# A recurrent attention kernel with a SoLU block behind it: another order for the blocks' inverses, and 32-blocks one round earlier

## The chip, the cores and the metric

The kernel runs on one core of a Trainium2 chip. The core has five engines that work in parallel, each through its own queue in program order: PE (TensorE, matrix products; PEld is its weight load), DVE (VectorE), ACT (ScalarE), POOL (GpSimd) and SP (SyncE, which here only issues transfers). They wait for one another through semaphores. Transfers between HBM and the core's SBUF are issued by SP, ACT or POOL and carried by 16 DMA engines. PE writes to PSUM, from which DVE or ACT must copy a result out before its bank can be used again.

The metric is the device time of one execution in microseconds. All inputs and outputs are 32-bit floats, or 64-bit for the weights that the kernel narrows itself.

## What is computed

A linear recurrence with a state of 40 x 40 for each of 4 x 8 heads and 768 positions, and behind it, on the 3072 rows of 320 that it gives, a block with a softmax-weighted hidden layer of 1024:

```python
for t in range(S):                                   # S = 768, D = 40
    y[:, :, t] = einsum('bhd,bhde->bhe', rt, state)
    Sa = einsum('bhde,bhe->bhd', state, at)
    state = state * wt[:, :, None, :] - einsum('bhd,bhe->bhde', Sa, bt)
    state = state + einsum('bhd,bhe->bhde', vt, kt)
...
h = x @ w_in                                         # 320 -> 1024
solu = h * softmax(h)
ln = (solu - mean(solu)) / sqrt(var(solu) + 1e-06) * g_ln
out = ln @ w_out                                     # 1024 -> 320
```

## The kernel before

**Tiling.** The 768 positions are cut into 12 chunks of L = 64. A *round* n is one chunk of all four batches; it holds two *steps*, i = 2n and 2n + 1, each with two batches, so there are 24 steps. Inside a chunk the recurrence becomes products, and the inverse of a triangular 64 x 64 matrix for each head. That matrix is called nt; its diagonal has two 32 x 32 blocks (Q = 32).

**The inverse.** The diagonal blocks of one round (64 heads and halves) are written to HBM by `scatter` (L424) and fetched again by `gather` as one block per partition. `invert` then eliminates column by column on DVE, two instructions for each column. For rounds below FINE = 4 (L23), `gather` (L434) and `invert_fine` work on blocks of 16: a set-up (L447, L448), then 14 pairs of L456 (prod) and L458 (u), two ACT copies (L462), and a write to HBM (L464). `solve` then has to join two 16-blocks on PE: products py16, DVE L602 (y), products pz16, and six ACT copies (L613, L618). From round FINE on, the blocks are 32 wide: `gather` by L439, set-up L476, L478, L480, then 30 pairs of L486 and L488, a write by L492, and nothing to join. Round 0's first step is inverted by doubling on PE instead, with DVE evictions L584, L589 and L593.

`bring_inverse(n)` (L499, four transfers on SP) brings round n's inverse into the one buffer tinvT. `solve` reads it first with a DVE transpose (L598) into tinv, then makes py and pz (L547), which ACT evicts (L629, L633).

**The order.** Nothing is left to a scheduler. Each stage is a generator, and `turns` takes a string of letters and advances the generator of each letter by one `yield`: f and g are `front` (decay factors and nt of a later step), a is `attend` (step i + 1: transposes kT, vT and rT, products psi and lamv, x), s is `solve` (step i + 1), I the inverse of a later round, r `recurrence` (step i), y `readout` (step i, ends with DVE L730), W the narrowing of the weights (L179 to L191), h `hidden`, o and b `output` and the rest of `hidden` for step i - LAG (LAG = 6). In `more` a letter has a count of yields, here `inverse_steps(i)` for I. Steps 0 to 5 use EARLY (L829; step 0 the second string, since it has two fronts), step 6 CENTRE (L832), later ones STEADY and LATE. So the order of instructions on every engine is written out by hand, and an instruction that waits holds up all behind it on its engine.

**Transfers.** `load(n, names)` issues two transfers for each of the inputs w, b, a, k, v, r of round n on SP (L335). In odd steps B stands for `arrivals`, which issues `bring_inverse` for the next round and then `gather` for the one after it; X is `repack` (L741 to L744), which turns the step's result into xT. At the end of step 0 the program has `scatter(2)`, then load(3, "k") and load(1, "r"); B of step 1 comes after them. `store` (L812) writes a round's output in two halves.

PSUM: transposes and small products share two banks ("bank"), so a product waits until the one two before it has been evicted; wide ones share two pairs of banks ("duo").

## Time and profile before

Five executions took 678.15 to 680.65 us, with a median of 679.33. The profiled execution took 675.67 us; its span from the first to the last instruction is 673.6 us.

| what | value |
|---|---|
| median of 5 executions | 679.33 us |
| profiled execution: time, span | 675.67 us, 673.6 us |
| mean granted TensorE clock | 0.968 of full speed |
| largest DMA queue (q1, issued by SP) | 45.80 MB, 39.9% of 16 engines' span |
| L488, DVE u, 32-blocks | x240, 66.6 us |
| L486, DVE prod, 32-blocks | x240, 65.8 us |
| L547, PE py | x1280, 24.1 us busy |
| DVE L598 waiting for tinvT by DMA | 27.7 us in 11 waits, longest 8.2 us |

The page also draws the span in 40 equal slices of 16.8 us; a digit is the busy share in tenths, and PEclk the granted clock:

```profile
PE   7697678798888999999999999999999999999996
PEld 4575566577666677677667667766766666555554
DVE  4549567487797696786887876976966844424433
ACT  3254545556445244334534433453442334412312
POOL 4414313132221121121112112111200100000000
PEclk9988867989899999999999999999999999999999
```

PE is busy nearly all the time from about the thirteenth slice on. In the first twelve, which hold the start-up and steps 0 to 6, it is not, and the clock is often below full speed. A step lasts 20 to 34 us in this part. Idle time of an engine costs something only where a chain of waits passes through it; the chain of work that ended last and the timeline say where.

### The profile page before, as it was taken

The numbers are of one execution on the slowest core, as the hardware profiler recorded it, in microseconds if no ns is written. First come the engines' busy times: TensorE is split into PE (matmuls) and PEld (weight loads), VectorE is DVE, ScalarE is ACT, GpSimd is POOL, SyncE is SP. The second block draws the span as 40 slices with busy tenths as digits, with TensorE's granted clock in tenths as the row PEclk, the third lists the DMA queues.
The fourth block names the chain that finished last, engine by engine and source line by source line (L and its number), as shares of the span: only waits on it lengthen the run. The fifth ranks groups of instructions, "written<-read, shape, count | busy, mean of one in ns | idle before, by whom it ended". The sixth has DMA issues, their size and how long they took to land.

```text
span 673.6 us, 28595 instructions
## 1 busy us (share of the span) xinstructions
PE 611.7 (91%) x12579; PEld 433.0 (64%) x12579; DVE 444.6 (66%) x1203; ACT 275.5 (41%) x663; POOL 119.1 (18%) x219
## 2 busy tenths in 40 slices
PE   7697678798888999999999999999999999999996
PEld 4575566577666677677667667766766666555554
DVE  4549567487797696786887876976966844424433
ACT  3254545556445244334534433453442334412312
POOL 4414313132221121121112112111200100000000
PEclk9988867989899999999999999999999999999999
DMA  9769648457362456454454543553334120000000
GB/s 157 107 149 151 120 82 134 90 110 134 84 105 50 97 80 119 66 97 86 74 93 88 89 80 84 84 93 82 39 76 78 25 42 19 21 24 20 19 21 19
DMA packets 238155, 53.74 MB, mean 80 GB/s; under 512 B 227400, under 2 KB 235344, under 8 KB 238032
## 3 DMA queue, kind: packets, MB, share of 16 engines
q1 hardware_dynamic: 232928, 45.80, 39.9%
q0 software_dynamic: 1696, 5.25, 3.1%
q8 instruction: 99, 1.62, 1.1%
q10 hardware_dynamic: 3408, 0.87, 0.9%
q14 instruction: 24, 0.20, 0.1%
HBM read 36.95 MB, written 10.22 MB: 70 GB/s over the span
## 4 chain that ended last, share of the span: by engine, by line
PE 67%; DVE 15%; ACT 8%; issue 5%; DMA 3%; SPq 1%; ACTq 1%; POOL 0%; DVEq 0%
PE po L799 16%; PE h L754 13%; PE pyo L723 4%; PE py L547 3%; PE pz L547 3%; PE plnT L794 3%; PE pcx L370 3%; DVE prod L486 2%; DVE u L488 2%; PE pcum L357 2%; PE plamv L308 2%; PE ppsi L308 2%; DVE nmax L764 2%; PE plamu L308 2%; DMA tinvT<-u_dram 2%
## 5 line engine op out<-in xcount | busy, mean ns | idle before, releaser
L754 PE MATMUL h<-w_in,xT 128*128 128x512 f32 (+1 forms) x288 | 124.9, 624 | 0.0
L799 PE MATMUL po<-w,lnT 128*128 128x320 f32 x384 | 115.9, 440 | 3.2 <-ACT lnT L795 3.2
L799 PEld LDWEIGHTS po<-w,lnT 128*128 128x128 f32 x384 | 68.3, 190 | 29.2 <-ACT lnT L795 5.8
L488 DVE TENSOR_TENSOR u<-u,prod 128x30 f32<-128x30 f32 (+7 forms) x240 | 66.6, 278 | 8.2
L486 DVE TENSOR_TENSOR prod<-blk,u 128x30 f32<-128x30 f32 (+7 forms) x240 | 65.8, 274 | 7.0
L764 DVE TENSOR_REDUCE nmax<-h 128x1 f32<-128x1024 f32 x24 | 29.3, 1221 | 52.5 <-PE h L754 52.5
L360 POOL TENSOR_TENSOR kx<-raw_b,inv 128x320 f32<-128x320 f32 x24 | 20.9, 869 | 232.6 <-ACT inv L358 218.7
L754 PEld LDWEIGHTS h<-w_in,xT 128*128 128x128 f32 (+1 forms) x288 | 38.0, 188 | 29.7 <-issue 27.7
L804 ACT ACTIVATE osb<-po,rs 128x320 f32<-128x320 f32 x24 | 12.6, 527 | 98.9 <-PE po L799 87.3
L795 ACT COPY lnT<-plnT 128x512 f32<-128x512 f32 x48 | 27.0, 587 | 41.2 <-PE plnT L794 41.1
L786 POOL TENSOR_TENSOR rs<-c,mhalf 128x1 f32<-128x1 f32 x24 | 13.2, 549 | 151.8 <-DVE c L785 150.7
L547 PE MATMUL py<-tinv,nt 32*32 32x32 f32 x1280 | 24.1, 200 | 15.7 <-DVE tinv L598 14.0
L311 DVE TENSOR_TENSOR lamv<-plamv,cst 128x512 f32<-128x512 f32 x24 | 16.6, 690 | 29.6 <-PE plamv L308 29.6
L771 DVE TENSOR_TENSOR e<-h,e 128x1024 f32<-128x1024 f32 x24 | 29.4, 1224 | 10.0 <-ACT e L768 9.4
L370 PE MATMUL pcx<-cst,lw 128*128 128x132 f32 x192 | 33.2, 300 | 3.1 <-DVE y L602 1.5
L768 ACT ACTIVATE e<-h,nmax 128x1024 f32<-128x1024 f32 x24 | 26.8, 1115 | 20.6 <-DVE nmax L764 15.3
L370 PEld LDWEIGHTS pcx<-cst,lw 128*128 128x128 f32 x192 | 27.5, 200 | 11.7 <-ACT y_mid L629 3.5
L633 ACT ACTIVATE tinvT<-pz 32x256 f32<-32x256 f32 x48 | 17.9, 373 | 39.9 <-PE pz L547 39.6
L372 ACT ACTIVATE kx<-pcx 128x264 f32<-128x264 f32 x48 | 18.8, 392 | 36.8 <-PE pcx L370 36.6
L547 PEld LDWEIGHTS py<-tinv,nt 32*32 32x32 f32 x1280 | 20.5, 113 | 20.3 <-issue 16.4
L709 POOL TENSOR_TENSOR sm<-tot,fac 128x320 f32<-128x320 f32 x20 | 14.8, 741 | 101.6 <-DVE tot L708 60.1
L730 DVE TENSOR_TENSOR x<-pyo,kx 128x512 f32<-128x512 f32 x24 | 16.2, 674 | 23.0 <-PE pyo L723 22.9
(139 smaller groups left out, 1192.5 us busy)
## 6 DMA issues: line engine op xcount, KB each, us to landing
blk<-blk_dram SPq DMA_DIRECT2D x16, 256.0 KB
raw_k<-in_k_dram SPq DMA_DIRECT2D x24, 160.0 KB
v<-in_v_dram SPq DMA_DIRECT2D x24, 160.0 KB
r<-in_r_dram SPq DMA_DIRECT2D x24, 160.0 KB
out_dram<-osb SPq DMA_DIRECT2D x24, 160.0 KB
raw_w<-in_w_dram SPq DMA_DIRECT2D x23, 160.0 KB
raw_b<-in_b_dram SPq DMA_DIRECT2D x23, 160.0 KB
raw_a<-in_a_dram SPq DMA_DIRECT2D x23, 160.0 KB
```

The source lines that it names most:

```text
L308: nc.tensor.matmul(t[half(c ^ p * cross), p, g * L:(g + 1) * L], lhsT=lhs[half(p), g, half(c)], rhs=rhs[half(p), g, half(c)], start=True, ...
L370: nc.tensor.matmul(t[:, g * 132:g * 132 + 132], lhsT=pair(lw, 2 * j + g), rhs=cst[:, lo:lo + 132], start=True, stop=True)
L486: nc.vector.tensor_tensor(out=t, in0=nb[:, j:j + 1, j + 1:Q].to_broadcast([P, rows, m]), in1=u[:, 0:rows, j:j + 1].to_broadcast([P, rows, ...
L488: nc.vector.tensor_tensor(out=u[:, 0:rows, j + 1:Q], in0=u[:, 0:rows, j + 1:Q], in1=t, op=ALU.subtract)
L547: nc.tensor.matmul(t[quarter(out), c:c + Q], lhsT=lhs(p, g), rhs=rhs(p, g), start=True, stop=True)
L723: nc.tensor.matmul(t[half(p), c, g * W:g * W + used], lhsT=kb[half(c), j, 2 * g + p, :], rhs=lam[half(c), h % 2, h // 2, 0:used], start=i ...
L754: nc.tensor.matmul(h[:, j * 512:j * 512 + 512], lhsT=of_round[i // 2]["xT"][rows, kt, i % 2 * P:i % 2 * P + P], rhs=w_in[rows, 4 if kt == ...
L764: nc.vector.tensor_reduce(out=nmax, in_=h, axis=AX.X, op=ALU.max, negate=True)
L768: nc.scalar.activation(out=e, in_=h, func=AF.Exp, bias=nmax, accum_out=esum)
L771: nc.vector.tensor_tensor(out=q, in0=h, in1=e, op=ALU.mult)
L795: nc.scalar.copy(out=lnT[:, fs.start:fs.stop].rearrange("p f t -> p (f t)"), in_=t)
L799: nc.tensor.matmul(o[:, 0:DM], lhsT=lnT[:, f, :], rhs=w2[:, f, :], start=f == 0, stop=f == NF - 1)
```

## The change

The diff touches the order and the size of blocks in the first third of the kernel and one transfer at the end:

- FINE becomes 3: round 3 (steps 6 and 7) is gathered, inverted and brought as 32-blocks, and solves 6 and 7 have nothing to join. `inverse_steps` gives 17 yields to step 3 and 15 to step 4, as the 32 yields need, where the 16-block inverse had 8 and 8.
- Load(3, "k") and load(1, "r") move from the end of step 0 into `arrivals` of step 1: k between `bring_inverse(1)` and `gather(2)`, r behind `gather(2)`.
- In step 0 the first yields of round 1's inverse stand behind one `a` and one `s` more, and there are 4 of them instead of 5, with 6 instead of 5 in the next place.
- In the start-up, `solve(0)` and the inverse of round 0 alternate otherwise, and one `s` moves from the third string into the second.
- CENTRE has two `s` less.
- The second half of the last round's store is issued by ACT.

```diff
-FINE = 4
+FINE = 3
...
-            nc.sync.dma_start(out=rows[:, 2 * c:2 * c + 2, :], in_=of_round[n]["osb"][half(c)])
+            (nc.scalar if c and n == NCH - 1 else nc.sync).dma_start(out=rows[:, 2 * c:2 * c + 2, :], in_=of_round[n]["osb"][half(c)])
...
-             "r r a r W f r r W g W s y r W a f g L W a I a s f g W a I s f g W I s a f g W I s f g W I")
+             "r r a r W f r r W g W s y r W a f g L W a a s I f g W a I s f g W I s a f g W I s f g W I")
...
-    CENTRE = "r r a r f o I r o r o s y o r X I o h a f L a s a h I f s a h I f s h f s h I a f h"
+    CENTRE = "r r a r f o I r o r o s y o r X I o h a f L a s a h I f a h I f s h f h I a f h"
...
         if i == 0:
-            return [5, 5, 5, 1, 0]
+            return [4, 6, 5, 1, 0]
...
         if i < LAG:
+            if i in (3, 4):
+                return [0, 0, 4, 4, 4, 5] if i % 2 else [5, 4, 4, 2, 0, 0]
             return [0, 0, 2, 2, 2, 2] if i % 2 else [3, 3, 1, 1, 0, 0]
...
             bring_inverse(n)
+        if i == 1:
+            load(3, "k")
         if n + 1 < NCH:
             gather(n + 1)
+        if i == 1:
+            load(1, "r")
...
-        turns("f g s f s * g a s f I s I f a s I g I s I g a I", dict(I=[2, 3, 3, 3, 3, 99]), f=f, g=g, s=so, a=at, I=inv,
+        turns("f g s f s * g a s f s I f a s I g I s I I g a s I", dict(I=[2, 3, 3, 3, 3, 99]), f=f, g=g, s=so, a=at, I=inv,
...
-        turns("s f W s * f a s a g s g f g W W", {}, f=f, g=g, s=so, a=at, W=ws, **{"*": warmer})
+        turns("f W s * f a s a g s g f g W W", {}, f=f, g=g, s=so, a=at, W=ws, **{"*": warmer})
...
-            if i == 0:
-                load(3, "k")
-                load(1, "r")
```

## The prediction

> **What bounds the kernel now.** I began with the page's busy shares and its chain of what ended last, since they say whether one engine or a relay of engines sets the end.

> ```profile
> PE 611.7 (91%) x12579; PEld 433.0 (64%) x12579; DVE 444.6 (66%) x1203; ACT 275.5 (41%) x663; POOL 119.1 (18%) x219
> ...
> PE 67%; DVE 15%; ACT 8%; issue 5%; DMA 3%; SPq 1%; ACTq 1%; POOL 0%; DVEq 0%
> ```

> PE holds two thirds of the chain, but DVE and DMA hold a fifth, and the 40 slices put their part in the first third. So I cut the span at L730, the last VectorE product of each step. L730 starts at 54.04 us in step 0, 88.10 in step 1, and so on to 222.32 in step 7. The busy times between these marks, in the order length, PE, PEld, DVE, ACT, POOL, granted clock, DMA share, GB/s:

> ```profile
> 88.10:111.50 23.40, 20.47 (x580) 17.30 (x581) 17.42 (x61) 11.88 (x34) 4.11 (x8) 0.72 0.66 111
> ...
> 134.28:154.59 20.31, 18.88 (x587) 15.04 (x588) 17.05 (x61) 11.31 (x33) 6.79 (x13) 0.92 0.56 111
> 154.59:175.82 21.23, 17.52 (x590) 13.85 (x587) 12.73 (x37) 12.84 (x35) 5.24 (x9) 1.00 0.69 135
> 175.82:197.05 21.23, 18.13 (x584) 14.75 (x586) 19.89 (x62) 9.51 (x26) 3.73 (x6) 0.92 0.43 80
> ...
> 222.32:246.57 24.25, 23.41 (x459) 16.72 (x460) 20.67 (x59) 9.89 (x23) 4.10 (x7) 1.00 0.53 94
> ```

> The last row shows that from step 8 PE is busy 23.41 of 24.25 us: time won or lost before 222 us reaches the end unchanged. In the fourth row DVE is busy 19.89 of 21.23 us; that step holds the start of the first 32-block inverse, and DVE sets its length. The second row is the step into which the change puts 32-blocks, and DVE is at 17.05 of 20.31 there already.

> Third, the timeline around the longest stall. Columns: start, length, engine, line, operation, count, idle time before it and its releaser.

> ```profile
> 76.02 1.37 SPq L335 DMA_DIRECT2D raw_k<-in_k_dram  x2
> 77.43 1.60 SPq L335 DMA_DIRECT2D r<-in_r_dram  x2
> 79.56 5.23 SPq L499 DMA_DIRECT2D tinvT<-u_dram  x4
> 84.83 2.02 SPq L434 DMA_DIRECT2D blk<-blk_dram  x2
> ...
> 87.46 0.71 DVE L598 STREAM_TRANSPOSE tinv<-tinvT 128x512 f32<-128x512 f32 x1 [8.16 <-DMA tinvT<-u_dram]
> ...
> 88.32 1.08 PE L547 MATMUL py<-tinv,nt 32*32 32x32 f32 x64 [8.87 <-DVE tinv L598]
> ...
> 91.57 1.11 PE L289 MATMUL prT<-cst,r 128*128 128x128 f32 x4
> ```

> SP issues four loads, then round 1's inverse; DVE waits 8.16 us for it, PE 8.87.

> **The change part by part.** The sum is made against the profiled execution (675.67 us, span 673.6) and then moved to the median, 679.33, which lies 3.66 higher.

> *Inverse of round 1 ahead of k(3) and r(1): -3.8 us.* L499 would start at 76.02. From first issue to L598, where L598 waited, took 6.4 us (127.23 to 133.65), 5.25 (169.93 to 175.18) and 3.3 (218.53 to 221.79), so L598 can run at 79.3 to 82.4 instead of 87.46. But what was ahead is now behind. The four L499 need 1.95 us to issue, the k loads 1.4, so gather L434 starts near 79.4. Its other awaited row took 4.8 us (22.23 to 27.07), so the blocks are there at 84.2, and L447, which stands in the DVE queue ahead of L602, waits for them. The r load starts near 81.4; k loads, the nearest rows for a landing, took 5.5 us (24.60 to 30.07) and 6.4 (76.02 to 82.38). With 6.4, since the queue is as full, prT runs at 87.8 instead of 91.57: -3.8. Behind prT on PE stand pz of solve 2 and all that follows, so prT decides. Bounds: L598 alone counts, at 79.3, -8.2; or r, now the last of the four, lands when the last of them, the gather, is used now (89.46), which leaves 2.1, of which the half clock takes 0.6: -1.5.

> *32-blocks in steps 3 and 4: +8.8 us.* Between the marks of steps 3 and 4 DVE has 13 pairs of L456 and L458 with the set-up L447. The changed DVE order has set-up L476 to L480 and 25 pairs of L486 and L488 in their place, everything else (four narrowed weight pieces, five masks) being the same. Old, start to start: 0.9 + 13 x 0.46 = 6.9 us. New, from the first 32-inverse in the trace: set-up 177.08 to 179.02, 1.9 us; 25 pairs from 0.45 us (128x30) to 0.65 (128x128), 14.3 us. DVE waited 2.3 us in the 20.31 (lamu 1.0, lamv 0.6, kx 0.5, nt 0.2) and was taken for the other 18.0. New length 18.0 - 6.9 + 16.2 = 27.3, +7.0; pairs that ran beside POOL took up to 0.8 longer (200 us), which gives up to +8.7. I take +7.3. The cover is only the 2.3 us of waits, and it is used up. After the mark, L602 of step 4 stood behind one pair (156.79 to 157.75); now behind four, 1.8 us plus the same stretch of 0.6: +1.5, and prT and pz wait for L602 there, so it passes on. Bounds 0 to 2.

> *The clock in the longer step: +0.8 us.* PE has no more work in 27 us, so it idles in pieces. Before 176.04 it idled 1.99 us, and the following row has clock 0.92, 1.7 us of full rate lost. One such drop may fall in steps 3 and 4, on PE's part of the chain or beside it: between 0 and two drops, 3.4; I take half of one.

> [...]

> *What steps 5 and 6 no longer do: -3.4 us.* Solves 6 and 7 lose py16, pz16, six ACT copies and L602, and their L598 moves 256 instead of 512 columns (0.44 against 0.71 us). The ACT copies are hidden. From 175.82 to 205 DVE does not wait, so each instruction counts: L598 twice and L602 twice, 0.26 each, 1.0. Then:

> ```profile
> 203.06 0.72 PE L370 MATMUL pcx<-cst,lw 128*128 128x132 f32 x4 [1.52 <-DVE y L602]
> ...
> 205.64 0.69 DVE L311 TENSOR_TENSOR lamv<-plamv,cst 128x512 f32<-128x512 f32 x1 [0.36 <-PE plamv L308]
> ...
> 210.97 1.22 DVE L764 TENSOR_REDUCE nmax<-h 128x1 f32<-128x1024 f32 x1 [2.03 <-PE h L754]
> ```

> PE's wait of 1.52 for L602 goes, with about 1.9 us of products (py16 0.6, pz16 1.3), so both DVE waits, 0.36 and 2.03, go too. 1.0 + 0.4 + 2.0 = 3.4; bounds 2 and 4.

> *Last store's second half on ACT's queue: -0.5 us.* After the last L804 the two L812 take 1.25 us to issue one behind the other; in parallel 0.6 is saved, bounds -0.65 and +0.3.

> *Nothing:* (a) Start-up and step 0. DVE gets the same instructions in another order up to L401 at 65.39, and DVE is full from 50 to 65. In the start-up L602 slips by some 0.6 us behind two more pairs, beside a paT that ends then anyway, and round 0's L464, two loads and L499 by 1.7; solve 1 reads the result only at 53.4. Bounds -1.0 and +0.8. (b) Gather 3 and round 3's u in other shapes: L439 issued in 1.93 us at 172.04, L434 took 3.10 at 129.34; L492 took 1.28 at 213.46, and SP waits at 162 to 167 for nt anyway. (c) The two "s" gone from CENTRE: solve 7 is exhausted by then.

> Sum: -3.8 + 7.3 + 1.5 + 0.8 - 3.4 - 0.5 = +1.9 us. 675.67 becomes 677.6; 679.33 becomes **681.2**.

> **The rivals.** *The round-1 stall goes whole (faster).* If blocks and r land by 83 us, prT follows py directly (3.2 us behind it, as now) and PE has no second idle, so that part of the low clock of 0.72 after the mark goes as well. The place is solve 2 in step 1, the price 8.2 and about 1 of clock, 9.2, and it decides from a gain of 5.7, r landing by 85.9. Then the sum with 7.3 + 1.5 - 3.4 - 0.5 and no clock term is -4.3: 675.0. For it: 8.16 us of wait is a lot, and SP's issue of L499 was slowed (5.23 against 1.95 elsewhere) by the loads ahead. Against it: the same slow queue now carries gather and r.

> *Round 3 loses the clock too (slower).* DVE-bound step 3 leaves PE at 18.9 of 27 us; after the mark of step 1 PE was at 20.5 of 23.4 and the clock still 0.72. Two drops on the path and the upper price of the pairs: +3.4 instead of 0.8 and +8.7 instead of 7.3 give +5.9: 685.2. Against it: step 5, also bound by DVE, kept 0.92.

> *The first part does nothing (slower).* The wait turns from L598 into L447 and prT, with r at 90.5 us: -1.0 instead of -3.8 gives +4.7: 684.0. For it: ten transfers (four L499, two each of k, blocks and r) must now land before prT, where eight did. Against it: the two rows of a k load say 5.5 and 6.4 us after issue, not 9.

> **How the numbers follow.** Within 0.2%, 1.4 us, is about what a measurement of this kernel can't tell from no change. Forecast 0.45, its own range 679 to 683.5; a third of it lies within 1.4 us. Whole stall gone 0.33, clock lost 0.15, first part idle 0.07. Faster 0.33; same 0.15; slower 0.30 + 0.15 + 0.07 = 0.52. The range reaches down to the first rival and up past the second: 674.9 to 686.0.

> **What would show it.** L598 of step 1 at 79 to 82 us, with L447 and prT waiting in turn for DMA. From the mark of step 3 to that of step 4 27 to 29 us, DVE without waits. Step 5 shorter by 0.5, step 6 by some 2.5 to 3. I am wrong if DVE's pairs in step 3 run beside waits larger than 2.3 us, or if prT starts before 85.

## The result, and the profile after

The changed kernel took 681.51 us in the median of 44 executions (675.80 to 685.98), the kernel before 678.81 in 79 that lay beside them (671.51 to 685.32). The ratio is 1.0049, 95% interval 1.0034 to 1.0063: 3.3 us slower (the two medians differ by 2.7). A single execution of either kernel scatters by a few us, so in what follows ratios are used for what a change is worth, and profiles for where the time lies. The profiled execution of the changed kernel took 683.05 us, with a span of 680.8.

From its page, the busy shares, the clock in 40 slices and the chain of what ended last:

```profile
PE 614.6 (90%) x12259; PEld 435.7 (64%) x12259; DVE 449.7 (66%) x1235; ACT 271.9 (40%) x649; POOL 118.4 (17%) x217
...
PEclk9889869798779999999999999999999999999999
...
PE 63%; DVE 18%; ACT 5%; issue 5%; SPq 4%; DMA 3%; ACTq 0%; POOL 0%; DVEq 0%; POOLq 0%
```

DVE's part of the chain rose from 15 to 18%, SP's queue from 1 to 4%, and the clock in the tenth to twelfth slice (153 to 204 us) fell from 9, 8 and 9 tenths to 8, 7 and 7. The time between the marks (L730 of one step to L730 of the next):

| steps | before | after | difference |
|---|---|---|---|
| start to 0 | 54.04 | 54.89 | +0.8 |
| 0 to 1 | 34.06 | 29.95 | -4.1 |
| 1 to 2 | 23.40 | 24.86 | +1.5 |
| 2 to 3 | 22.78 | 23.17 | +0.4 |
| 3 to 4 | 20.31 | 27.08 | +6.8 |
| 4 to 5 | 21.23 | 25.55 | +4.3 |
| 5 to 6 | 21.23 | 22.09 | +0.9 |
| 6 to 7 | 25.27 | 22.49 | -2.8 |
| 9 to 23 | 323.24 | 322.95 | -0.3 |

The busy times of the changed kernel in these stretches; columns: start and end, length, PE, PEld, DVE, ACT, POOL with their instructions, granted clock, DMA share, GB/s:

```profile
84.84:109.70 24.86, 19.76 (x583) 16.39 (x583) 17.56 (x61) 11.91 (x35) 4.98 (x9) 0.76 0.66 109
132.87:159.95 27.08, 20.03 (x592) 15.36 (x591) 24.56 (x86) 11.95 (x35) 6.29 (x11) 0.94 0.56 106
159.95:185.50 25.55, 22.45 (x586) 18.45 (x586) 14.05 (x44) 12.00 (x33) 5.25 (x9) 0.73 0.53 96
185.50:207.59 22.09, 16.88 (x424) 13.54 (x426) 19.12 (x61) 8.05 (x21) 3.56 (x6) 0.85 0.44 75
207.59:230.08 22.49, 20.91 (x451) 15.12 (x452) 18.11 (x47) 9.56 (x22) 4.03 (x7) 1.00 0.47 79
```

The second row (step 3 to 4) has DVE busy 24.56 of 27.08 us, where it had 17.05 of 20.31: that is the 32-block inverse. The third row (step 4 to 5) is the surprise. DVE has 14.05 us to do in 25.55, PE is busy 22.45 at a clock of 0.73; before, the same step had PE at 17.52 us and a clock of 1.00. PE has about as many products as before (586 against 590) and is busy 4.9 us longer with them.

The timeline of the changed kernel around round 1; columns: start, length, engine, line, operation, count, idle time before it and its releaser:

```profile
77.15 3.69 SPq L499 DMA_DIRECT2D tinvT<-u_dram  x4
80.89 1.39 SPq L335 DMA_DIRECT2D raw_k<-in_k_dram  x2
82.38 2.10 SPq L434 DMA_DIRECT2D blk<-blk_dram  x2
84.20 0.71 DVE L598 STREAM_TRANSPOSE tinv<-tinvT 128x512 f32<-128x512 f32 x1 [4.80 <-DMA tinvT<-u_dram]
84.52 1.66 SPq L335 DMA_DIRECT2D r<-in_r_dram  x2
85.06 1.07 PE L547 MATMUL py<-tinv,nt 32*32 32x32 f32 x64 [5.58 <-DVE tinv L598]
86.32 0.86 POOL L360 TENSOR_TENSOR kx<-raw_k,inv 128x320 f32<-128x320 f32 x1 [4.41 <-DMA raw_k<-in_k_dram]
87.13 0.29 DVE L447 TENSOR_SCALAR u<-blk 128x256 f32<-128x256 f32 x1 [0.84 <-DMA blk<-blk_dram]
90.50 1.08 PE L289 MATMUL prT<-cst,r 128*128 128x128 f32 x4 [2.12 <-DMA r<-in_r_dram]
```

L598 came at 84.20 instead of 87.46, with a wait of 4.80 instead of 8.16 us. But L447 now waits for the blocks and prT for r, and prT starts at 90.50 instead of 91.57. Measured from the mark of step 0 it came 1.9 us earlier. POOL's L360, which reads k of round 3, now waits 4.41 us for it; POOL's next instruction then waits 1.89 us for DVE, so nothing on POOL is held up by that.

### The profile page after: what moved, and what is told of

It is laid out like the page before. It is cut to its first block, busy times and chain, and to the rows that moved or that the text cites. A ratio compares the mean times of both kernels' runs of the same rounds, so it can differ in the third digit from the quotient of the medians.

```text
span 680.8 us, 27973 instructions
## 1 busy us (share of the span) xinstructions
PE 614.6 (90%) x12259; PEld 435.7 (64%) x12259; DVE 449.7 (66%) x1235; ACT 271.9 (40%) x649; POOL 118.4 (17%) x217
## 3 DMA queue, kind: packets, MB, share of 16 engines
q0 software_dynamic: 1696, 5.25, 3.1%
## 4 chain that ended last, share of the span: by engine, by line
PE 63%; DVE 18%; ACT 5%; issue 5%; SPq 4%; DMA 3%; ACTq 0%; POOL 0%; DVEq 0%; POOLq 0%
PE po L799 16%; PE h L754 13%; PE pyo L723 4%; DVE prod L486 4%; DVE u L488 3%; PE plnT L794 3%; PE pcx L370 2%; PE pz L547 2%; PE py L547 2%; PE pcum L357 2%; DVE nmax L764 2%; PE plamv L308 2%; PE ppsi L308 2%; PE pyo L645 2%; PE plamu L308 2%
## 5 line engine op out<-in xcount | busy, mean ns | idle before, releaser
L754 PE MATMUL h<-w_in,xT 128*128 128x512 f32 (+1 forms) x288 | 124.9, 624 | 0.0
L488 DVE TENSOR_TENSOR u<-u,prod 128x120 f32<-128x120 f32 (+4 forms) x270 | 73.9, 274 | 9.3
L486 DVE TENSOR_TENSOR prod<-blk,u 128x120 f32<-128x120 f32 (+4 forms) x270 | 74.1, 274 | 7.8
L764 DVE TENSOR_REDUCE nmax<-h 128x1 f32<-128x1024 f32 x24 | 29.3, 1220 | 50.4 <-PE h L754 50.4
L360 POOL TENSOR_TENSOR kx<-raw_b,inv 128x320 f32<-128x320 f32 x24 | 21.0, 874 | 238.9 <-ACT inv L358 211.0
L754 PEld LDWEIGHTS h<-w_in,xT 128*128 128x128 f32 (+1 forms) x288 | 38.0, 188 | 29.7 <-issue 27.7
L804 ACT ACTIVATE osb<-po,rs 128x320 f32<-128x320 f32 x24 | 12.7, 527 | 98.6 <-PE po L799 87.1
L311 DVE TENSOR_TENSOR lamv<-plamv,cst 128x512 f32<-128x512 f32 x24 | 16.5, 688 | 32.0 <-PE plamv L308 32.0
L547 PE MATMUL py<-tinv,nt 32*32 32x32 f32 x1152 | 23.1, 200 | 14.5 <-DVE tinv L598 7.8
L370 PE MATMUL pcx<-cst,lw 128*128 128x132 f32 x192 | 33.3, 302 | 0.8 <-ACT vT L291 0.5
L370 PEld LDWEIGHTS pcx<-cst,lw 128*128 128x128 f32 x192 | 27.9, 202 | 8.7 <-ACT y_mid L629 3.7
L547 PEld LDWEIGHTS py<-tinv,nt 32*32 32x32 f32 x1152 | 19.6, 114 | 18.8 <-issue 9.3
L776 DVE BATCH_NORM_STATS2 bs<-e 128x6 f32<-128x512 f32 x48 | 30.8, 684 | 0.6
L730 DVE TENSOR_TENSOR x<-pyo,kx 128x512 f32<-128x512 f32 x24 | 16.1, 673 | 22.3 <-PE pyo L723 22.2
```

The costliest lines, as they stand in the source:

```text
L370: nc.tensor.matmul(t[:, g * 132:g * 132 + 132], lhsT=pair(lw, 2 * j + g), rhs=cst[:, lo:lo + 132], start=True, stop=True)
L486: nc.vector.tensor_tensor(out=t, in0=nb[:, j:j + 1, j + 1:Q].to_broadcast([P, rows, m]), in1=u[:, 0:rows, j:j + 1].to_broadcast([P, rows, ...
L488: nc.vector.tensor_tensor(out=u[:, 0:rows, j + 1:Q], in0=u[:, 0:rows, j + 1:Q], in1=t, op=ALU.subtract)
L547: nc.tensor.matmul(t[quarter(out), c:c + Q], lhsT=lhs(p, g), rhs=rhs(p, g), start=True, stop=True)
L754: nc.tensor.matmul(h[:, j * 512:j * 512 + 512], lhsT=of_round[i // 2]["xT"][rows, kt, i % 2 * P:i % 2 * P + P], rhs=w_in[rows, 4 if kt == ...
L764: nc.vector.tensor_reduce(out=nmax, in_=h, axis=AX.X, op=ALU.max, negate=True)
```

## The experiments

Ratios are always to the kernel before, taken beside the same runs, with 95% intervals; they are not the quotients of the medians.

### Which part costs: the change without 32-blocks, the 32-blocks alone, the loads alone

```diff
(the changed kernel, no 32-blocks in round 3)
-FINE = 3
+FINE = 4
-            if i in (3, 4):
-                return [0, 0, 4, 4, 4, 5] if i % 2 else [5, 4, 4, 2, 0, 0]
```

> The changed kernel with 16-blocks in round 3 again (32-blocks from round 4 on, as before); the moved loads, the start-up orders, CENTRE and the last store stay as changed. Theory A (the steps of the prediction: the loads gain, the 32-blocks of steps 3 and 4 cost more than steps 5 and 6 give back): the loads -3.8 by the prediction's sum, or about -2.2 by the marks of the two profiles (step 0 to 1 -4.1, the two steps behind it +1.9), the store -0.5, so 674.5 to 676.6 us, ratio to the kernel before 0.993 to 0.996; step 3 to 4 back at 20 to 21 us and step 6 to 7 back at 25. Theory B (the 32-blocks are neutral in the whole and the loss is in the loads and the start-up, where half clock moved from one place to another): as slow as the changed kernel, 681 us or more, ratio 1.003 or more.

Measured: 675.39 us, ratio 0.9971 (0.9948 to 0.9994). Step 3 to 4 took 21.41 us and step 6 to 7 24.41. Without the 32-blocks the change is a gain of 2.0 us, so theory B is out; the gain is smaller than theory A had it, whose range the interval still reaches.

```diff
(the kernel before, 32-blocks in round 3 alone)
-FINE = 4
+FINE = 3
+            if i in (3, 4):
+                return [0, 0, 4, 4, 4, 5] if i % 2 else [5, 4, 4, 2, 0, 0]
```

> The kernel before with 32-blocks in round 3 and their step lists alone. Theory A: step 3 to 4 takes 27 us (+7), step 4 to 5 2 to 4 longer with half clock behind the late L602, step 6 to 7 some 2.8 shorter: +5.2 by the prediction's terms (7.3 + 1.5 - 3.4, with no clock), up to +8 with the clock that the marks show, so 684.5 to 687.5 us, ratio 1.008 to 1.012. Theory B: the 32-blocks give back what they take: ratio 0.998 to 1.002.

Measured: 681.56 us, ratio 1.0066 (1.0032 to 1.0100), 4.5 us. Its busy times from the marks of steps 3, 4 and 6, columns as above:

```profile
130.17:158.70 28.53, 21.22 (x592) 16.66 (x592) 25.63 (x87) 11.93 (x35) 6.43 (x11) 0.88 0.63 116
158.70:180.62 21.92, 19.06 (x583) 15.38 (x584) 14.14 (x45) 11.39 (x32) 5.24 (x9) 0.84 0.48 88
...
202.69:225.20 22.51, 20.70 (x451) 15.19 (x452) 18.12 (x47) 9.57 (x22) 4.03 (x7) 1.00 0.51 90
```

DVE fills step 3 to 4 again, and step 6 to 7 is again 2.8 us shorter; the first is far larger than the second. Theory A is right in kind, its lower end a little high. Its 2 to 4 us for step 4 to 5 are not in this profile: the step took 21.92 us, 0.7 longer than before, at a clock of 0.84, although PE waited as long for L602 as in the changed kernel:

```profile
163.79 0.77 PE L547 MATMUL pz<-tinvT,y 32*32 32x32 f32 x63 [2.26 <-DVE y L602]
```

```diff
(the kernel before, the two loads moved as in the change)
@@ arrivals
             bring_inverse(n)
+        if i == 1:
+            load(3, "k")
...
             gather(n + 1)
+        if i == 1:
+            load(1, "r")
@@ end of step 0
-                load(3, "k")
-                load(1, "r")
```

> The kernel before with only k of round 3 and r of round 1 moved behind the inverse of round 1. Theory A: L598 of step 1 at 80 to 84 us, prT waits for r; -3.8 by the prediction's sum, about -2 if the new wait for r keeps PE at half clock and the steps 1 to 3 give half of it back; 675.5 to 677.3 us, ratio 0.9945 to 0.997. Theory B: the wait only changes its name, prT no earlier than 90.5 us and the mark of step 3 where it was: ratio 0.999 to 1.002.

Measured: 677.15 us, ratio 1.0031 (0.9999 to 1.0064). (The medians, 677.15 beside 677.88, differ a little the other way; the 3.8 us of the prediction would be a ratio of 0.9944.) Neither theory had this: L598 and prT came earlier, and the kernel was not measurably faster. The timeline of this kernel:

```profile
81.67 0.71 DVE L598 STREAM_TRANSPOSE tinv<-tinvT 128x512 f32<-128x512 f32 x1 [4.24 <-DMA tinvT<-u_dram]
82.34 1.64 SPq L335 DMA_DIRECT2D r<-in_r_dram  x2
84.93 0.29 DVE L447 TENSOR_SCALAR u<-blk 128x256 f32<-128x256 f32 x1 [1.17 <-DMA blk<-blk_dram]
88.14 1.09 PE L289 MATMUL prT<-cst,r 128*128 128x128 f32 x4 [2.29 <-DMA r<-in_r_dram]
```

The same two new waits as in the changed kernel. Step 0 to 1 took 29.03 us (-5.0), step 1 to 2 25.03 (+1.6) at a clock of 0.75, and step 4 to 5 25.37, where the profile before has 21.23. So the moved loads by themselves bring no gain that could be measured, where the prediction had -3.8.

### Why step 4 grew: the late L602, or the clock behind it

In the changed kernel PE waited 2.26 us for L602 in step 4 (it belongs to solve 5, which runs there). The wait, and the granted clock in the stretches around it:

```profile
165.03 1.08 PE L547 MATMUL pz<-tinvT,y 32*32 32x32 f32 x64 [2.26 <-DVE y L602]
```

```profile
161.70:165.10 3.40, 1.14 (x42) 0.84 (x37) 3.16 (x12) 0.94 (x2) 1.77 (x3) 1.00 0.34 68
165.10:178.70 13.60, 13.60 (x309) 11.70 (x310) 6.50 (x22) 6.43 (x19) 1.69 (x4) 0.50 0.39 75
```

For 3.40 us PE was busy a third of the time; for the 13.60 us after that it ran at half clock without a pause. Two experiments take this apart. The first removes what made L602 late, four pairs ahead of it on DVE:

```diff
(the changed kernel)
-                return [0, 0, 4, 4, 4, 5] if i % 2 else [5, 4, 4, 2, 0, 0]
+                return [0, 0, 4, 4, 4, 5] if i % 2 else [5, 4, 0, 6, 0, 0]
```

> The changed kernel with one difference: in step 4 the pairs of round 3's second half come behind L602 of solve 4 instead of four of them ahead of it. Theory A (PE's 2.26 us of wait for L602 at 165.0 us brings the 13.6 us of half clock behind it, and so most of the 4.3 us by which step 4 to 5 grew): the wait under 1 us, no half clock from 165 to 179, step 4 to 5 at 21.5 to 23.5 us; -2 to -4 against the changed kernel, 677.5 to 679.5 us, ratio to the kernel before 0.998 to 1.001. Theory B (step 4 is longer because DVE has more to do in it, wherever the pairs stand): the pairs only move, step 4 to 5 stays at 25 us or the nt that round 3's inverse waits for comes later and step 5 grows by as much; ratio 1.004 to 1.006 as the changed kernel.

Measured: 677.59 us, ratio 1.0007 (0.9976 to 1.0038), against 1.0049 for the changed kernel: 2.9 us less, give or take 2.3 by the two intervals. Its steps 3 to 4 and 4 to 5:

```profile
129.82:157.05 27.23, 20.00 (x592) 15.44 (x591) 24.53 (x87) 11.97 (x35) 6.28 (x11) 0.94 0.58 112
157.05:174.96 17.91, 16.31 (x583) 13.30 (x584) 13.73 (x44) 11.35 (x32) 5.25 (x9) 1.00 0.65 118
```

DVE has the same work, step 3 to 4 the same length, and step 4 to 5 falls from 25.55 to 17.91 us, further than expected, at full clock. One profile overstates it: the two profiled executions differ by 9.8 us (673.23 and 683.05), the ratios by 2.9.

The second experiment leaves L602 as late as it was and only gives PE something to do in the wait:

```diff
(the changed kernel, in solve, ahead of pz16; the products are read by nobody)
+            if i == 5:
+                for _ in range(5):
+                    nc.tensor.matmul(idle[:, 0:256], lhsT=ident, rhs=cst[:, 0:256], start=True, stop=True)
             t = products("pz16", ...
```

> The changed kernel with five 128x256 products into an unused half of a PSUM tile put on PE's queue ahead of pz16 in step 4, where PE waited 2.26 us for L602 (about 1.9 us by the 0.38 us that such a product takes). DVE's order and the wait for L602 stay. Theory A (the wait costs its own 1.5 us and, through the half clock that follows a stretch of PE at 34%, some 3 more): half clock from 165 to 179 gone, step 4 to 5 at 21 to 23.5 us instead of 25.55, -1.5 to -3 against the changed kernel, ratio to the kernel before 1.000 to 1.003. Theory B (the wait alone counts, the clock falls for other reasons): step 4 to 5 stays at 25 us, ratio 1.004 to 1.006.

Measured: 679.65 us, ratio 0.9998 (0.9968 to 1.0028), 3.5 us less than the changed kernel, give or take 2.3. From its timeline, and its busy times in step 4 to 5:

```profile
164.53 2.32 PE L608 MATMUL idle<-cst 128*128 128x256 f32 x10
166.96 0.72 PE L547 MATMUL pz<-tinvT,y 32*32 32x32 f32 x62
```

```profile
161.87:181.68 19.81, 18.48 (x593) 15.10 (x594) 14.14 (x45) 11.33 (x32) 5.25 (x9) 1.00 0.60 103
```

With five useless products (recorded as ten), 2.32 us long, the step is 5.7 us shorter in this profile: pz takes 0.72 us where it took 1.08, and the clock is 1.00. pz starts 5.1 us after the mark in both kernels (165.03 against 159.95, 166.96 against 161.87), so what the step lost, it lost behind pz. That speaks for theory A: the wait costs more than its own length, through the clock behind it.

How much of it is clock is less sure. Step 4 to 5 also took 25.37 us in the profile of the loads alone and 25.52 in that of the start-up orders below, with 6.8 and 10.2 us at half clock and no late L602, so the length of this step in one profile proves little; the two ratios carry the argument. Over all their executions the mean clock was 0.958 in both variants (12 each) and 0.955 in the changed kernel (44). By these numbers some 4 us less of the span passed at half clock (an estimate, 2 x 0.003 x 680), not 13.6; and the kernel before differs as much between the chips of these runs (0.962 to 0.967).

### What keeps the round 1 stall from being won

Here nothing stands between the scatter and round 1's inverse, and r comes a step earlier:

```diff
(the kernel before)
-        load(1, "v")
+        load(1, "v", "r")
...
-                parts["L"] = later((i + 6) // 2, *("bk" if i else "b"))
+                parts["L"] = later((i + 6) // 2, "b", "k")
...
-            if i == 0:
-                load(3, "k")
-                load(1, "r")
```

> The kernel before with r of round 1 loaded along with v of round 1 at the start of step 0, and k of round 3 loaded in the middle of step 0 behind b of that round: nothing then stands between the scatter of round 1's y and its inverse, and r is there before prT asks. Theory A (in the changed kernel the stall of step 1 turned into a wait for r and for the blocks, so only some 2.6 to 3.4 us of the 8.16 came out by the mark of step 2): L598 at 79 to 82 us, prT at 84 to 87 and waiting for no load, the mark of step 2 at 103 to 106 us, -5 to -8 against the kernel before, ratio 0.988 to 0.993. Theory B (what is won in step 1 goes again into half clock of steps 2 and 3): ratio 0.997 or more although prT starts by 87.

Measured: 671.45 us, ratio 0.9906 (0.9877 to 0.9935), 6.4 us less than before. Its timeline:

```profile
77.70 3.35 SPq L499 DMA_DIRECT2D tinvT<-u_dram  x4
81.21 1.69 SPq L434 DMA_DIRECT2D blk<-blk_dram  x2
84.35 0.71 DVE L598 STREAM_TRANSPOSE tinv<-tinvT 128x512 f32<-128x512 f32 x1 [5.62 <-DMA tinvT<-u_dram]
86.35 0.29 DVE L447 TENSOR_SCALAR u<-blk 128x256 f32<-128x256 f32 x1
88.46 0.97 PE L289 MATMUL prT<-cst,r 128*128 128x128 f32 x4
89.36 0.72 PE L547 MATMUL pz<-tinvT,y 32*32 32x32 f32 x62
```

L598 comes no earlier than in the changed kernel (84.35), and prT at 88.46, outside of what theory A said. But neither L447 nor prT waits for a load, and step 1 to 2 takes 20.95 us at a clock of 0.90, where the changed kernel had 24.86 at 0.76. The gain of theory A is there, by another way than it named.

Which of the two loads counts? The next kernel has r early, and k where the changed kernel has it:

```diff
(the run with the loads alone)
-        if i == 1:
-            load(1, "r")
...
-        load(1, "v")
+        load(1, "v", "r")
```

> The kernel before with r of round 1 loaded along with v of round 1, and k of round 3 where the changed kernel has it, behind the inverse of round 1. It differs from the run with the loads alone only in r, and from the run that takes both earlier only in k. Theory A (prT and with it r decides, and the blocks only come next): L447 waits some 1 us for the blocks, prT for no load, half clock behind py no longer than two stretches of 3.41 us; ratio 0.990 to 0.995, near the 0.9906 of both loads earlier. Theory B (the k loads, which push the gather of the blocks back, take the gain whatever r does): ratio 0.998 to 1.003, as the loads alone.

Measured: 679.58 us, ratio 0.9992 (0.9960 to 1.0024). Timeline, and step 1 to 2:

```profile
80.38 1.90 SPq L335 DMA_DIRECT2D raw_k<-in_k_dram  x2
82.38 2.75 SPq L434 DMA_DIRECT2D blk<-blk_dram  x2
88.00 1.11 PE L289 MATMUL prT<-cst,r 128*128 128x128 f32 x4
88.24 0.29 DVE L447 TENSOR_SCALAR u<-blk 128x256 f32<-128x256 f32 x1 [2.26 <-DMA blk<-blk_dram]
89.79 1.08 PE L547 MATMUL pz<-tinvT,y 32*32 32x32 f32 x64 [0.68 <-ACT rT L291]
```

```profile
84.53:109.90 25.37, 23.33 (x583) 19.59 (x583) 17.66 (x62) 12.00 (x35) 4.97 (x9) 0.62 0.55 94
```

prT waits for nothing any more and starts at 88.00, and still nothing is won. The place of k of round 3 alone separates 0.9992 from 0.9906: theory B's ratio. Its reason, the late blocks, is not shown. They do land later, and L447 waits 2.26 us for them, but up to pz this costs PE nothing: pz, which needs L602 and so stands behind L447, waits for ACT's copy of prT, and it starts 34.41 us after the mark of step 0, with both loads early 34.73. The difference lies behind pz, where PE runs at half clock: 20.5 us in one stretch from 83.4 us on, 6.8 with both loads early. Over the executions the mean clock was 0.959 here and 0.970 there, and 0.963 and 0.967 in the kernel before beside them.

The profiles of the other kernels agree on the place, if not on the reason. From the mark of step 0 to that of step 2 it is 51.3 to 52.0 us in the three kernels with both loads early (the two of "Together" below included), 53.8 to 56.2 in the six with k behind round 1's inverse, and 54.9 to 57.5 in the three with the loads as before (kernels with products put into this wait left out). The half clock behind the stall lasts 6.8 us in each of the first three, 13.6 or more in five of the six, and 10.2 in each of the last three. Why k behind the inverse prolongs it is open.

### The start-up and the orders alone

The kernel before with the new strings of the start-up, of step 0 and of CENTRE (the diff of the change without FINE, `inverse_steps` for 3 and 4, the loads and the store).

> The kernel before with the orders of the start-up, of step 0 and of CENTRE from the changed kernel alone (no moved loads, no 32-blocks, the store as before). The prediction put these at nothing, bounds -1.0 and +0.8: ratio 0.9985 to 1.0012, mark of step 0 at 53 to 55 us. Theory B (they are what made the changed kernel without 32-blocks 2.0 us faster, where the loads alone showed no gain): ratio 0.995 to 0.998.

Measured: 675.54 us, ratio 0.9964 (0.9939 to 0.9989): 2.4 us less, nearer to theory B. The profile does not say clearly where. The mark of step 0 is at 54.51 us (+0.5). Step 5 to 6 is 0.6 longer and step 6 to 7 0.9 shorter, so CENTRE brings about nothing. Step 1 to 2 takes 21.34 (-2.1) and step 2 to 3:

```profile
109.42:129.18 19.76, 16.48 (x582) 13.54 (x583) 12.42 (x37) 12.04 (x34) 5.75 (x10) 1.00 0.61 122
```

This is 3.0 us less than before, at full clock; but step 4 to 5 then took 25.52 us, 4.3 more. In one profile such gains and losses of the clock can't be told from chance, and the next runs do not repeat the gain.

### Together, and against the clock

With the loads as in the run that takes r and k earlier, once on the changed kernel without 32-blocks, once on the changed kernel with L602 ahead of the pairs:

> The changed kernel without the 32-blocks of round 3 and with the loads as in the run that takes r and k earlier. Theory A: -2.0 as the changed kernel without 32-blocks, and 3 to 5 more from the rest of the stall; ratio 0.989 to 0.993. Theory B (half clock behind it takes the gain back): 0.996 to 0.998.

> The changed kernel with the pairs of step 4 behind L602 and with the loads as in the run that takes r and k earlier. Theory A: as the run with the pairs behind L602 (1.0007), and 3 to 5 us from the rest of the stall; ratio 0.993 to 0.997, some 2 us behind the same kernel with 16-blocks, since step 3 to 4 keeps its 27 us and step 6 to 7 gives 2.8 back. Theory B (with the pairs behind L602 the 32-blocks cost nothing more): no slower than the one with 16-blocks, 0.990 to 0.993.

Measured: 671.65 us, ratio 0.9925 (0.9894 to 0.9956), and 672.39 us, 0.9924 (0.9894 to 0.9954). Neither is distinguishable from the early loads alone (0.9906), so no gain of the start-up orders is seen on top of them. And the two agree, as theory B of the second has it, though its interval reaches into theory A's range. Its step 3 to 4 took 27.97 us, step 4 to 5 18.52 and step 6 to 7 22.82, against 20.49, 21.72 and 25.00: the 7.5 us come back as 3.2 and 2.2, and the rest is within the scatter.

Last, products into PE's idle time ahead of py16 of solve 2 (fifteen with the loads early, twenty on the kernel before; the edit is that of the filled wait above, ahead of py16 and for i == 2):

> The run that takes r and k earlier, with fifteen 128x256 products (5.7 us) on PE's queue ahead of py16 of solve 2, where PE idled 6.27 us for L598. Theory A: the half clock from 82.3 to 89.1 goes, the step from mark 1 to 2 is 1 to 2 us shorter, ratio 0.986 to 0.990 against 0.9906 without. Theory B: no change in the clock, or the products run longer than the wait and push py16 back: ratio 0.990 to 0.994.

> The kernel before with twenty 128x256 products (7.6 us) on PE's queue ahead of py16 of solve 2, where PE idled 8.87 us for L598; the loads stay where they were. Theory A: the half clock from 84.2 to 94.4, three stretches of 3.41 us, goes, -2 to -4 us, ratio 0.994 to 0.997, so a part of what the stall costs is clock and not wait. Theory B: ratio 0.999 to 1.002.

Measured: with the early loads 671.57 us, ratio 0.9892 (0.9847 to 0.9938), the lowest ratio of all and not distinguishable from 0.9906; the half clock behind py is gone (full from 74.5 to 112.1 us), but step 2 to 3 took 25.08 us instead of 20.41. On the kernel before 678.15 us, 0.9980 (0.9946 to 1.0015): step 1 to 2 fell from 23.40 to 20.18 us, and step 2 to 3 rose to 26.79. In these two profiles filling moved the half clock on rather than away. Over the executions it did not: on the kernel before, the mean clock was 0.969 with the products and 0.962 without, some 9 us less at half clock by the same estimate. The time fell by only 1.4 us, give or take 2.4, so what half clock costs behind this stall stays open.

## Why the prediction came out as it did

The forecast was 681.2 us, +1.9; measured were 681.51 and +3.3. The sum was near, but that it came so near is luck: several of its terms were wrong by 1.5 to 6 us, with opposite signs.

- **The bound.** Right: from the mark of step 9 to that of step 23 it is 323.24 and 322.95 us, and what was won or lost ahead reached the end.
- **Inverse of round 1 ahead of k(3), r(1): -3.8.** Wrong. The loads alone gave 1.0031 (0.9999 to 1.0064), no gain. The step that failed is "so prT decides". In the run with r early prT waited for no load and came earlier than with both loads early (32.6 against 33.8 us after the mark of step 0), and the ratio was 0.9992 against 0.9906. What was won up to prT was lost behind it, at half clock, which the term left out but for 0.6 us in one bound. Only with the k loads off SP's queue behind the inverse was the stall worth something. The issue times were also too short: I gave the four L499 1.95 us and L598 79.3 to 82.4; they took 3.69, and L598 came at 84.20. r took 6.0 us where I had 6.4, but was issued 3.1 us later than I had it, so prT stood at 90.50. That is the r of 90.5 in the rival "the first part does nothing", which I held for the least likely; in this one term it described the trace.
- **Step 3 to 4: 27.3 us, bound by DVE.** Right: 27.08, and 28.53, 27.23, 27.11 and 27.97 in the other four kernels with 32-blocks in round 3, whose loads and orders differ. DVE's waits there were 0.39 and 0.53 us and little more.
- **L602 of step 4 late by 1.5.** Right: it came 4.7 us after the mark instead of 3.2, and PE waited 2.26 us for it.
- **The clock: +0.8.** The mechanism was right, the size too small. With L602 just as late and only the wait filled, 3.5 us went, give or take 2.3 (1.0049 to 0.9998). That is about the upper bound of 3.4, two drops, from which I took half of one; in the profile the drop was one stretch of 13.6 us, not of 3.4, behind a gap of 2.26 us on PE.
- **Steps 5 and 6: -3.4.** Step 6 to 7 gave the 2.8 predicted. Step 5 to 6 grew by 0.9 where I had -0.5: PE, without py16 and pz16, waited 1.62 us for L191 and 2.16 for L401 there, and the clock was 0.85 instead of 0.92. Together -1.9, just short of the bound of 2.
- **The 32-blocks in the whole** were +6.2 in the sum (7.3 + 1.5 + 0.8 - 3.4) and measured +4.5 alone, and +5.3 as the difference between the changed kernel with and without them.
- **Start-up, step 0, CENTRE: nothing.** Too high: 0.9964 (0.9939 to 0.9989) is -2.4, beyond the bound of -1.0, though the interval reaches -0.7. For CENTRE alone the marks agree with nothing. What in the start-up or step 0 brings it, and whether it is more than the clock falling elsewhere, is open: beside the early loads no gain was seen.
- **The store: -0.5.** Small and of that sign: from the last L730 to the end of the span the six kernels with the ACT store have 80.3 to 80.6 us (mean 80.4), the eight without 80.5 to 80.7 (mean 80.6), a gain of 0.2.

- **The rivals.** For the whole stall to go, r had to be there by 85.9; it was used at 90.50. The rival in which step 3 loses the clock had the mechanism, one step early: the clock of step 3 to 4 was 0.94, that of step 4 to 5 0.73.

Measured alone, the parts are +2.1 (loads), +4.5 (32-blocks), -2.4 (orders) and -0.2 (store), +4.0 together, each of the first three give or take 2; the sum had -3.8, +6.2, 0 and -0.5. The gain that the loads did not bring was made up in part by that of the orders, and by 32-blocks that cost less than I had.

## What to carry to other kernels

Price a wait on PE by what follows it as well: here five useless products in 2.3 us of idle, or the late instruction moved ahead of four others on DVE, brought about 3 us. It is no rule: twenty products in 8.9 us of idle brought nothing that could be measured. When a transfer is moved past others on a queue, measure each one's place by itself: the place of k, which no wait on PE pointed to, separated 0.9992 from 0.9906, while moving r alone out of the wait that did show (1.0031 to 0.9992) brought nothing that could be measured. A sum that comes out right says little about its terms; one run for each part does.

## What the hardware showed that was not expected

| PE busy in the window | clock full, next window half | clock half, next window still half |
|---|---|---|
| under 40% | 33 of 33 | 9 of 9 |
| 40 to 50% | 22 of 29 | 3 of 3 |
| 50 to 60% | 22 of 44 | 7 of 7 |
| 60 to 70% | 7 of 82 | 5 of 5 |
| 70 to 90% | 0 of 425 | 30 of 30 |
| 90% and more | 0 of 1876 | 41 of 125 |

In these profiles it went by how little PE did within one window more than by the length of one gap: of the six windows at 50 to 60% and full clock in the kernel before and the changed kernel, the three with the longest gaps (1.52 to 1.55 us) were followed by half clock once, the three with shorter ones (1.19 to 1.51 us) each time. Six are few. Full clock came back only behind windows at 90% and more, 84 of 125, and behind none of the 54 others at half clock. Where the grid cut a gap of 2 us in two, the clock could stay full: in the kernel before, 2.01 us at 18.5 us lay across windows of 71 and 65% and was followed by full clock (1.88 us at 59.6 us, across 67 and 53%, by half clock), while 1.99 us at 174.1 us lay in one window of 42% and the 2.26 us of the changed kernel in one of 34%, both followed by half clock. This may be a large part of the scatter, but was not tested by itself. Windows in which PE was busy for 40 to 60% were followed by half clock in 44 of 73 cases. It is a count over profiles, and PE's ends are modelled; why some full windows at half clock were followed by another is not explained.

**The scatter goes with the clock.** Over 35 executions of the kernel before, the time falls by 4.3 us for each 0.01 of mean clock (correlation -0.85). The mean clock was 0.955 in the changed kernel's 44 executions, 0.966 in those 35, and 0.962 to 0.967 in the kernel before on the four chips of the experiments.
